# Chunked attention and a bilinear FFN on one core: x's sums ahead of ab's sums on GpSimd, one earlier transposition, one later output part

## The chip, the cores and the metric

The kernel runs on one core of a Trainium2 chip. The metric is the device time of one execution in microseconds. Before the change its median is 300.36 us over 5 runs (299.89 to 300.96).

Five engines work side by side, each through its own instructions in the order written: TensorE (PE for matmuls, PEld for the loads of the operand that stays in the array), VectorE (DVE), ScalarE (ACT), GpSimd (POOL) and SyncE (SP), which issues the DMAs. They meet through semaphores.

## The reference

Attention inside chunks of 64 tokens, then a feed-forward layer without an activation: two projections, multiplied with each other, and an output projection.

```python
q_c = q.reshape(B, H, nc, 64, D)            # B 8, H 8, S 576, D 64; k_c, v_c alike
scores = np.matmul(q_c, k_c.transpose(0, 1, 2, 4, 3)) / np.sqrt(D)
attn = np.exp(scores - scores.max(-1, keepdims=True))
attn = attn / (attn.sum(-1, keepdims=True) + 1e-09)
attn_out = np.matmul(attn, v_c).reshape(B, H, S, D)
x = attn_out.transpose(0, 2, 1, 3).reshape(B * S, H * D)   # 4608 x 512
out = ((x @ w_a) * (x @ w_b)) @ w_out       # d_ff 1536, out 4608 x 512
```

## The kernel before

The 4608 tokens are 9 blocks (`K`, 0 to 8) of 512, and 18 units (`U`) of 256; block K holds units 2K and 2K+1. The order of each engine's work is written out by hand: what is emitted first for an engine is in front in its queue.

**A unit's attention.** `load` brings q, k and v (SP), `cast` (line 211) makes them bf16, nearly always on GpSimd, and q and k are transposed: on TensorE in `transpose_pe` (line 224) for the first units, by DMA in `transpose_dma` afterwards. `bring` (line 383) is casts of q and k, loads of the next unit, DMA transpositions. Then follow `scores` (matmuls, exponentials on ACT), `sums` (matmuls with ones, logarithms on ACT), `inverse` (ACT) and `values` (line 335), whose matmuls leave attention's values in PSUM; DVE multiplies them with the inverse sums into the block's transposed `xT` (line 356, two instructions for a unit).

**The projections from block 2 on** use a seven-product scheme (Strassen and Winograd) in place of eight, for each of six groups `Group(K, i)` (line 493) of 256 columns of w_a and w_b. It needs four sums of parts of x, `s1` to `s4`: `combine_x` (line 477), on GpSimd from block 3 on, emitted in the preceding block at `i == 5`. They need both units' `xT`. A group's products `p1, p6, p2, p5, p7` run in its own iteration, `p3` and `p4` in the next one. `p6` is the first that reads a sum (`s2`). `p1`'s result is copied by ACT from PSUM bank pa to pb (line 529), and `p6` adds onto the copy. `p3` and `p4` end with DVE multiplications (line 561) that write `ab`, the product of the two projections.

**The output projection** of block K-1 runs while block K is projected, again with seven products: `OutGroup(K-1)` (line 602) has parts `(n, th)`, n from 0 to 6 and th 0 or 1, six matmuls each, in this order. It needs sums of parts of ab: `combine_ab` (line 573), on GpSimd, whose parts 0, 1 and 2 are emitted for one third `j` of the columns at a time, and part 3 for all thirds together in the next block. The part with `n == 2` has s2 of ab as the operand that is loaded into the array; its six loads take two for each third. The parts with `n` 0 and 1 add into one bank, po; between them ACT copies po to pq (line 675, after part (0, 1)), and n = 2 and 3 add onto that copy.

**The main loop** (from line 984) goes over K from 2 to 8 and over the six groups i. In one iteration, in this order: casts and `bring`s, `p1`, the preceding group's `add7` on DVE, `chunk(c0)`, the preceding group's `p3`, attention of place (K, i, 0) with `combine_x` at i = 5, `p6`, the preceding group's `p4`, `finish(last)`, `p2`, `chunk(c1)`, attention of place (K, i, 1), `p5`, `exps`, `chunk(c2)`, `p7`. `chunk(n)` emits the next n output parts; the counts stand in the table `chunks` (line 969), two entries for an iteration, c0 and then c1, or a pair (c1, c2). `finish(g)` (line 977) emits the three `combine_ab` instructions of third i - 3 when the group that it is handed has i of 3, 4 or 5. So a block's thirds of ab's sums are emitted at i = 4, at i = 5 and at i = 0 of the next block.

**Block 0** (line 814) is projected directly, in pairs of 128-column tiles: `b_of(0)`, `b_of(1)`, `a_of(0)`, `a_of(1)`; pair 4 also holds the transposition and the scores of unit 2.

Of the kernel before, what the change touches and what calls it, by code (L numbers as in the profile page):

```python
# [16 lines left out]
def kernel(  # L17
# [28 lines left out]
    NBLK = NTOK // BLK  # L46
# [41 lines left out]
    def bank(pool=None):  # L88
        if pool is None:
            pool = spread[0]  # L90
            spread.append(spread.pop(0))
        if pool is psum_b:
            pool = psum_b[0]
            psum_b.append(psum_b.pop(0))
        return pool.tile([128, 512], FP32, name=bank_names[id(pool)])
# [59 lines left out]
    def combine_wo(part, j):  # L155
        k = slice(2 * j, 2 * j + 2)
        k2 = slice(HFT + 2 * j, HFT + 2 * j + 2)
        b11, b12 = wo_sb[:, k, 0:256], wo_sb[:, k, 256:512]
        b21, b22 = wo_sb[:, k2, 0:256], wo_sb[:, k2, 256:512]
        t1, t2, t3, t4 = [t[:, k] for t in wo_t]  # L160
        o, x0, x1, op = (
            (t3, b22, b12, SUB), (t2, t3, b11, ADD), (t4, b21, t2, SUB), (t1, b12, b11, SUB)
        )[part]
        nc.gpsimd.tensor_tensor(out=o, in0=x0, in1=x1, op=op)
# [46 lines left out]
    def cast(U, names="qkv"):  # L211
        for n in names if U < NU else "":
            if U >= 4 and wo_sums:
                combine_wo(*wo_sums.pop(0))
            raw[n, U] = raw_pool.tile(
                [128, 2, H, D], BF16, name=f"{n}_raw"
            )
            eng = nc.vector if U == 0 and n != "v" else nc.gpsimd
            eng.tensor_copy(out=raw[n, U], in_=staged.pop((n, U)))
# [4 lines left out]
    def transpose_pe(U, names="qk"):  # L224
        if U not in qkt:
            qkt[U] = qkt_pool.tile([128, 2, 2, NKT, 128], BF16, name="qkt")
        for n in names:
            w = "qk".index(n)
            src = raw.pop((n, U))
            t = [bank() for _ in range(2 if U < 3 else 1)]  # L230
            tp = [
                t[i % len(t)].bitcast(BF16).rearrange("c (i m p) -> c i m p", i=2, m=NKT)[:, i]
                for i in range(2)
            ]
            for i in range(2):
                for m in range(NKT):
                    nc.tensor.transpose(
                        tp[i][:, m, :],
                        src[:, i, 2 * m:2 * m + 2, :].rearrange("p j d -> p (j d)"),
                        identity,  # L240
                    )
            dst = qkt[U][:, w].rearrange("c g m (p i) -> c i m g p", i=2)
            for i in range(2):
                on_dve = i == 0 if U in (0, 2) else w == 0 or U == 1
                cp = nc.vector.tensor_copy if on_dve else nc.scalar.copy
                cp(out=dst[:, i], in_=tp[i].rearrange("c m (g p) -> c m g p", g=2))
# [51 lines left out]
    def sums(U, halves=None, pools=(None, None)):  # L298
        E = E_of[U]
        sm = [bank(p) for p in pools]  # L300
        for cl in range(2):
            for j in range(2):
                nc.tensor.matmul(
                    sm[cl][j * 64:j * 64 + 64, :],
                    ones[cl * 64:cl * 64 + 64, :],
                    E[cl * 64:cl * 64 + 64, j].rearrange("p m g s -> p (m g s)"),
                    start=True,
                    stop=True,
                )
        ln_of[U] = sm_pool.tile([128, 2, NKT, 128], FP32, name="ln")  # L310
        rs_of[U] = ln_of[U]
        ln = ln_of[U]
        for cl in range(2):
            late_ln.append(
                lambda cl=cl: nc.scalar.activation(
                    out=ln[:, cl].rearrange("p m n -> p (m n)"), in_=sm[cl], func=AF.Ln
                )
            )
        for cl in range(1 if pools[0] else 2):
            late_ln.pop(0)()  # L320
            if halves:
                inverse(U, cl)

    def inverse(U, cl=None):

        if (U, cl) == (1, 1):
            for m in (slice(0, 2), slice(2, 4)):
                nc.scalar.activation(
                    out=rs_of[U][:, 1, m], in_=ln_of[U][:, 1, m], func=AF.Exp, scale=-1.0
                )  # L330
            return
        c = slice(0, 2) if cl is None else cl
        nc.scalar.activation(out=rs_of[U][:, c], in_=ln_of[U][:, c], func=AF.Exp, scale=-1.0)
# [49 lines left out]
    def bring(U, names="qkv"):  # L383

        if U >= NU:
            return
        cast(U, "qk")
        load(U + 1, "q" if U < 9 else "qkv")
        transpose_dma(U)
        if "v" in names:  # L390
            bring_v(U)
# [345 lines left out]
    with tc.manual_schedule(  # L737
# [72 lines left out]
        def combo():  # L810
            if combos:
                combine_w(*combos.pop(0))

        for i in range(NWP):
            pair = Pair(i) if i else first
            pair.b_of(0, (None,) if i else (1,), i == 5)
            if i == 5:
                sums(2, halves=True)
            pair.b_of(1, (None,) if i else (1,), i >= 4)
            if i == 4:  # L820
                transpose_pe(2)
                pair.copy(1)
            if i == 5:
                values(2)
                pair.copy(0)
                pair.copy(1)
            pair.a_of(0)
            if i == 4:
                scores(2)
            if 1 <= i < 5:  # L830
                combo()
            pair.a_of(1)
            if 0 <= i < 5:
                combo()
# [129 lines left out]
        def attend(K, i, n):  # L964
# [3 lines left out]
        last = None  # L968
        chunks = {
            2: (1, 1, 1, 1, 1, 2, 1, 2, 3, 0, 1, 1),  # L970
            3: (1, 1, 1, 1, 2, 1, 1, 2, 2, 0, 1, 1),
            4: (1, 0, 1, 2, 1, (1, 1), 1, 2, 2, 0, 1, 1),
            5: (1, 1, 1, 1, 1, (1, 1), 1, 2, 2, 0, 1, 1),
            NBLK - 1: (1,) * 12,
        }
# [1 line left out]
        def finish(g):  # L977

            K, i = g.K, g.i
            if K >= 2 and i >= 3:  # L980
                for part in (0, 1, 2):
                    combine_ab(K, part, i - 3, nc.vector if (K, i) == (NBLK - 1, 5) else None)

        for K in range(2, NBLK):
            for i in range(NWP):
                if i == (2 if K == 2 else 1):
                    for j in range(3):
                        combine_ab(K - 1, 3, j)
                if K == 2 and i in (1, 3):
                    bring((8, 9)[i // 2], ("qkv", "qk")[i // 2])  # L990
                elif K == 3 and i in (1, 3, 5):
                    bring(10 + i // 2, ("qkv", "qkv", "qk")[i // 2])
                elif K > 3 and i == 1:
                    bring(2 * K + 5, "qk")
                elif K > 3 and i == 2:
                    cast(2 * K + 4, "v")
                elif K > 3 and i == 3:
                    cast(2 * K + 5, "v")
                    bring(2 * K + 6, "qk")
                if i == 0:  # L1000
                    g = OutGroup(K - 1)
                    outs += [
                        lambda g=g, n=n, th=th: g.part(n, th) for n in range(7) for th in range(2)
                    ]
                now = Group(K, i)
                steps = chunks.get(K, chunks[5])[2 * i:2 * i + 2]
                c0, c1, c2 = steps[0], *(steps[1] if type(steps[1]) is tuple else (steps[1], 0))
                now.p1()
                while late_ln:
                    late_ln.pop(0)()  # L1010
                if last:
                    last.add7()
                chunk(c0)
                if K == 2 and i == 0:
                    for j in range(3):
                        combine_wo(3, j)
                if last:
                    last.p3()
                attend(K, i, 0)
                now.p6()  # L1020
                if last:
                    last.p4()
                    finish(last)
                if K == 2 and 0 < i < 4:
                    combine_w(i + 2, 3)
                if K == 2 and i == 4:
                    cast(9, "v")
                now.p2()
                chunk(c1)
                attend(K, i, 1)  # L1030
                now.p5()
                exps()
                chunk(c2)
                now.p7()
                last = now
        ends = [
            OutGroup(NBLK - 1, 0, (psum_t, psum_q, psum_c)),
            OutGroup(NBLK - 1, 1, (psum_t, psum_b, psum_a)),
# [44 lines left out]
```

## Time and profile before

| What | Value |
|---|---|
| Median of 5 runs (lowest, highest) | 300.36 us (299.89, 300.96) |
| The profiled execution's own time | 300.82 us |
| Its span, first to last instruction | 299.0 us |
| PE busy | 289.8 us, 97% |
| PEld busy | 232.6 us, 78% |
| POOL busy | 217.5 us, 73% |
| DVE busy | 197.9 us, 66% |
| ACT busy | 196.7 us, 66% |
| Granted TensorE clock | 1.00 |

The span is what the engines' instructions cover; the execution's own time is 1.8 us longer. An engine's share is an average over all stages. A row of the timeline has the start in us, the time in us, engine, line, operation, what is written and read, the shape, how many like it follow one another (their time is that of all together), and in brackets how long the engine sat idle before it and what ended that.

### The profile page before, as it was taken

How to read it: one execution, taken by the hardware profiler on the slowest of the kernel's cores; microseconds unless marked ns; L12 is line 12 of the kernel's file. 1: busy time of each engine (PE TensorE's matmuls, PEld its weight loads, DVE VectorE, ACT ScalarE, POOL GpSimd, SP SyncE). 2: the span in 40 equal slices, each digit the busy share in tenths (PEclk: the TensorE clock that was granted, in tenths of full speed). 3: DMA queues.
4: the chain of work that ended last, by engine and by line, in shares of the span. 5: the costliest groups of instructions: out<-in, count | busy, mean ns of one | idle time of the engine just before them, and what ended most of it. 6: DMA issues, size and time to landing. Idle time of an engine off the chain costs nothing.

```text
span 299.0 us, 8610 instructions
## 1 busy us (share of the span) xinstructions
PE 289.8 (97%) x3531; PEld 232.6 (78%) x3531; DVE 197.9 (66%) x312; ACT 196.7 (66%) x357; POOL 217.5 (73%) x203
## 2 busy tenths in 40 slices
PE   7799999999999999999999999999999999999995
PEld 3354478766688888887888888888888888888884
DVE  3656777867787765676466756675667576765672
ACT  2743477268587767874977687768776876566622
POOL 0557669999899499939993999299819922992660
PEclk9999999999999999999999999999999999999999
DMA  7999999999999979999999983980313001100025
GB/s 228 312 366 366 309 354 352 248 203 199 275 244 163 240 168 263 179 238 235 217 263 226 267 198 68 233 198 2 72 45 89 12 2 70 73 2 0 2 99 183
DMA packets 141159, 54.29 MB, mean 182 GB/s; under 512 B 117184, under 2 KB 135232, under 8 KB 141120
## 3 DMA queue, kind: packets, MB, share of 16 engines
q1 hardware_dynamic: 140976, 53.69, 72.9%
q8 instruction: 27, 0.44, 0.6%
q14 instruction: 12, 0.10, 0.1%
q10 hardware_dynamic: 144, 0.07, 0.1%
HBM read 37.75 MB, written 9.44 MB: 158 GB/s over the span
## 4 chain that ended last, share of the span: by engine, by line
PE 87%; SPq 3%; POOL 3%; ACT 3%; DMA 2%; issue 1%; DVE 1%; DVEq 0%; POOLq 0%
PE pb L511 18%; PE pc L511 11%; PE pa L511 11%; PE po L654 11%; PE pq L654 10%; PE pb L435 4%; PE pb L727 3%; PE pq L417 2%; PE pa L417 2%; DMA st<-in_moe_w_b_dram 2%; PE po L435 2%; PE po L417 2%; PE pt L345 2%; PE pc L417 2%; SPq L188 2%; PE pc L435 1%
## 5 line engine op out<-in xcount | busy, mean ns | idle before, releaser
L591 POOL TENSOR_TENSOR so<-ab_sb 128x512 f16<-128x512 f16 x23 | 26.6, 1156 | 42.9 <-DVE ab_sb L561 42.9
L511 PEld LDWEIGHTS <-t 128*128 128x128 f16 x504 | 48.7, 98 | 8.4 <-issue 2.8
L549 DVE TENSOR_TENSOR c_sb<-pc,v_sb 128x512 f32<-128x512 f32 x42 | 29.0, 691 | 35.6 <-ACT v_sb L522 35.6
L511 PE MATMUL pb<-s,wa 128*128 128x256 f16 x336 | 50.6, 273 | 0.1
L511 PE MATMUL pa<-xT,wb 128*128 128x256 f16 x336 | 50.4, 273 | 0.0
L654 PEld LDWEIGHTS <-ab_sb 128*128 128x128 f16 x390 | 37.8, 98 | 4.3
L522 ACT COPY u_sb<-pb 128x512 f32<-128x512 f32 x42 | 24.7, 587 | 19.4 <-PE pb L511 19.2
L561 DVE SCALAR_TENSOR_TENSOR ab_sb<-pc,c_sb 128x512 f16<-128x512 f32 x42 | 29.0, 691 | 10.8 <-PE pc L511 10.2
L511 PEld LDWEIGHTS <-wa 128*128 128x128 f16 x336 | 31.7, 98 | 5.4 <-issue 1.6
L511 PEld LDWEIGHTS <-wb 128*128 128x128 f16 x336 | 32.9, 98 | 3.9
L561 DVE SCALAR_TENSOR_TENSOR ab_sb<-pb,b_sb 128x512 f16<-128x512 f32 x42 | 29.0, 691 | 6.7 <-PE pb L511 5.7
L529 ACT COPY pb<-pa 128x512 f32<-128x512 f32 x42 | 23.9, 570 | 11.7 <-PE pa L511 11.5
L654 PEld LDWEIGHTS <-so 128*128 128x128 f16 x288 | 28.2, 98 | 3.3
L522 ACT COPY b_sb<-pa 128x512 f32<-128x512 f32 x42 | 24.9, 592 | 8.0 <-PE pa L511 8.0
L550 DVE TENSOR_TENSOR pc<-pc,u_sb 128x512 f32<-128x512 f32 x42 | 29.0, 689 | 0.0
L522 ACT COPY v_sb<-pb 128x512 f32<-128x512 f32 x42 | 24.6, 586 | 5.0 <-PE pb L511 4.9
L591 POOL TENSOR_TENSOR so<-so,ab_sb 128x512 f16<-128x512 f16 x23 | 26.6, 1155 | 1.7
L591 POOL TENSOR_TENSOR ab_sb<-ab_sb 128x512 f16<-128x512 f16 x23 | 26.9, 1171 | 0.0
L356 DVE TENSOR_TENSOR xT<-pt,ln 128x512 f16<-128x512 f32 x31 | 20.2, 686 | 9.3 <-PE pt L345 7.2
L591 POOL TENSOR_TENSOR so<-ab_sb,so 128x512 f16<-128x512 f16 x23 | 26.1, 1161 | 0.0
L511 PE MATMUL pb<-s,t 128*128 128x256 f16 x168 | 25.3, 273 | 0.8 <-POOL s L491 0.7
L511 PE MATMUL pc<-xT,t 128*128 128x256 f16 x168 | 25.2, 273 | 0.1
(148 smaller groups left out, 585.0 us busy)
## 6 DMA issues: line engine op xcount, KB each, us to landing
st<-in_v_dram SPq DMA_DIRECT2D x32, 256.0 KB, 4.5
out_dram<-o_sb SPq DMA_DIRECT2D x30, 256.0 KB, 2.5
st<-in_k_dram SPq DMA_DIRECT2D x22, 256.0 KB, 4.1
st<-in_q_dram SPq DMA_DIRECT2D x20, 256.0 KB, 3.9
st<-in_q_dram SPq DMA_DIRECT2D x6, 512.0 KB, 5.9
st<-in_moe_w_b_dram SPq DMA_DIRECT2D x6, 512.0 KB, 7.5
st<-in_moe_w_a_dram SPq DMA_DIRECT2D x6, 512.0 KB, 7.1
st<-in_moe_w_out_dram SPq DMA_DIRECT2D x6, 512.0 KB, 6.4
```

The lines of the kernel that those rows point to most:

```text
L356: nc.vector.tensor_tensor(out=x.rearrange("p m (g c s) -> p m g c s", g=2, c=2)[:, m, :, cl, :], in0=av[cl][:, m], in1=rs[:, cl, m].rearra ...
L417: nc.tensor.matmul(ps[n], w_ab[n, i][:, kt, o:o + 128], xT[:, kt, c0:c1], start=(kt == 0), stop=(kt == NKT - 1),)
L435: nc.tensor.matmul(t[:, c], w_ab[n, i][:, kt, o:o + 128], x_tiles[0][:, kt, c], start=(kt == 0), stop=(kt == NKT - 1),)
L511: nc.tensor.matmul(t[:, h * 256:h * 256 + 256], w[:, kt, h * 128:h * 128 + 128], x[:, kt], start=start and h == 0 and kt == 0, stop=h == 1 ...
L522: nc.scalar.copy(out=t, in_=src)
L529: nc.scalar.copy(out=self.B, in_=self.A)
L549: nc.vector.tensor_tensor(out=self.c, in0=self.C, in1=self.v, op=ADD)
L550: nc.vector.tensor_tensor(out=self.C, in0=self.C, in1=self.u, op=ADD)
L561: nc.vector.scalar_tensor_tensor(out=self.dst[:, :, c0:c0 + 256], in0=t.rearrange("p (h n) -> p h n", h=2), scalar=AB_SCALE, in1=o.rearran ...
L591: (eng or nc.gpsimd).tensor_tensor(out=o, in0=x0, in1=x1, op=op)
L654: nc.tensor.matmul(t[:, c0:c0 + 256][:, cols], a[:, kt, th * 128:th * 128 + 128], w[:, kt, cols], start=n in (0, 4) and first and kt == 0, ...
L727: nc.tensor.matmul(out_ps[K, tg], ab_tiles[K][:, ft, tg * 128:tg * 128 + 128], wo_sb[:, ft], start=(ft == 0), stop=(ft == NFT - 1),)
```

## The change

Three edits. First, in blocks 2 to 7 the first third of ab's sums is no longer emitted at i = 4 but at i = 5, together with the second third and after `combine_x` of the next block; and the cast of v of unit 9, which stood at i = 4 of block 2, follows `combine_x` too. The last block keeps its order. Second, in block 0's pair 4 the q of unit 2 is transposed on TensorE between the two b products, and its k where both were. Third, in block 4 the second output part goes from i = 1 to i = 0, behind `p5`, and iteration 1 has one part before and one after the attention in place of one and two.

```diff
@@ -816,9 +816,11 @@
             pair.b_of(0, (None,) if i else (1,), i == 5)
             if i == 5:
                 sums(2, halves=True)
+            if i == 4:
+                transpose_pe(2, "q")
             pair.b_of(1, (None,) if i else (1,), i >= 4)
             if i == 4:
-                transpose_pe(2)
+                transpose_pe(2, "k")
                 pair.copy(1)
             if i == 5:
                 values(2)
@@ -969,7 +971,7 @@
         chunks = {
             2: (1, 1, 1, 1, 1, 2, 1, 2, 3, 0, 1, 1),
             3: (1, 1, 1, 1, 2, 1, 1, 2, 2, 0, 1, 1),
-            4: (1, 0, 1, 2, 1, (1, 1), 1, 2, 2, 0, 1, 1),
+            4: (1, (0, 1), 1, 1, 1, (1, 1), 1, 2, 2, 0, 1, 1),
             5: (1, 1, 1, 1, 1, (1, 1), 1, 2, 2, 0, 1, 1),
             NBLK - 1: (1,) * 12,
         }
@@ -1020,11 +1022,14 @@
                 now.p6()
                 if last:
                     last.p4()
-                    finish(last)
+                    if K == 2 and i == 5:
+                        cast(9, "v")
+                    if i == 5 and K < NBLK - 1:
+                        finish(before)
+                    if i != 4 or K == NBLK - 1:
+                        finish(last)
                 if K == 2 and 0 < i < 4:
                     combine_w(i + 2, 3)
-                if K == 2 and i == 4:
-                    cast(9, "v")
                 now.p2()
                 chunk(c1)
                 attend(K, i, 1)
@@ -1032,7 +1037,7 @@
                 exps()
                 chunk(c2)
                 now.p7()
-                last = now
+                before, last = last, now
```

## The prediction

> **What bounds the kernel now.** I read the page, the chain of waits, PE's own waits, and then timelines around each edit. The chain says 87% PE, and busy PE is 97%.
>
> ```profile
> PE 87%; SPq 3%; POOL 3%; ACT 3%; DMA 2%; issue 1%; DVE 1%; DVEq 0%; POOLq 0%
> ...
> PE pb L511 <- POOL s L491: 0.7, 1, 0.7
> ...
> 138.88 1.15 POOL L491 TENSOR_TENSOR s<-s,xT 128x512 f16<-128x512 f16 x1
> ...
> 140.08 0.60 PE L511 MATMUL pb<-s,t 128*128 128x256 f16 x4 [0.70 <-POOL s L491]
> ```
>
> After the start-up, PE's matmuls follow one another at their own pace (0.109 us from one 256-column matmul to the next), so what a matmul waits is lost for good, and what no matmul waits for costs nothing. From start to start I find three places after 17 us that this change touches. **C**, at 139.1: p6 of block 4's first group waits for s2 of x; the group before it starts at 138.78 and needs 0.44, so p6 could start at 139.22; it starts at 140.08, 0.86 late. **A**, at 34.5: unit 2's scores wait for ACT's copy of the transposed k. **D**, at 144.8: p6 of block 4's second group waits for ACT's copy pb<-pa; p3 before it starts at 144.05, so 144.49 would do: 0.31 late.
>
> Ahead of each block, POOL's row tells what sets C:
>
> ```profile
> 132.22 1.16 POOL L591 TENSOR_TENSOR so<-ab_sb 128x512 f16<-128x512 f16 x1 [4.78 <-DVE ab_sb L561]
> ...
> 135.66 1.05 POOL L219 CAST q_raw<-st 128x1024 bf16<-128x1024 f32 x1
> 136.63 1.05 POOL L219 CAST k_raw<-st 128x1024 bf16<-128x1024 f32 x1
> 137.64 1.16 POOL L491 TENSOR_TENSOR s<-xT 128x512 f16<-128x512 f16 x1
> ```
>
> POOL sits idle for 4.78 us with the casts of unit 12 queued behind ab's first third, which waits for DVE; then come two casts, then x's sums.
>
> **What the Trainium skill says.** "PSUM — Partial Sum Buffer", section "Engine vs sequencer instructions": the queues of ScalarE, VectorE and GpSimd are strict FIFO. The trace agrees: the 4.78 us idle above, with k of unit 12 landed at 132.9. The same page, section "PSUM bank collisions raise a hardware error", has PSUM guarded by bank: so a matmul that adds into po must let ACT's copy of po end first; in the trace part (1, 0) of block 4 starts at 146.1, after the copy of 145.15 to 145.76. "Perfetto Trace Analysis", section "Identifying the Most-Contended Engine", warns that matmul busy time isn't distance from the limit; hence start to start above (weight loads are busy 78% here).
>
> **Part 1, x's sums first (POOL).** Nothing is added; 3 instructions of 1.16 (ab's first third) go behind 4 of 1.16 (x's sums).
>
> *Block 3 to 4.* The casts of unit 12 no longer stand behind the third. Its q landed at 131.0 and k at 132.9: casts end at about 134.0, x's sums need xT (DVE done at 133.55), so they start near 134.1 and s2 is done 2.4 later, at 136.5, against the need at 139.22. C goes: **-0.86**. All nine ab instructions end no later than before, since the casts use the idle time. DMA: the transpositions of unit 12 stand behind loads on SP that end at 143.1, so an earlier cast doesn't move them.
>
> *The other blocks.* No casts stand there, and here the edit has a price: x's sums wait for the second unit's xT, later than the DVE multiplication that ab's third waited for.
>
> ```profile
> 102.22 1.16 POOL L591 TENSOR_TENSOR so<-ab_sb 128x512 f16<-128x512 f16 x1 [0.48 <-DVE ab_sb L561]
> ...
> 115.93 1.15 POOL L591 TENSOR_TENSOR so<-so,ab_sb 128x512 f16<-128x512 f16 x1
> ...
> 102.27 1.29 DVE L356 TENSOR_TENSOR xT<-pt,ln 128x512 f16<-128x512 f32 x2
> ...
> 117.25 0.75 PEld L654 LDWEIGHTS <-so 128*128 128x128 f16 x7
> ```
>
> Rows 1 and 2: POOL at the end of block 2 starts at 102.22 and ends s2 of ab's last third at 115.93 + 1.15 = 117.08, without a pause. Row 3: xT is done at 103.56, so x's sums can start at 103.65 (0.09 from DVE's end to POOL's start, as at 132.13 to 132.22). The same set of instructions, v9's cast included, starts 1.43 later with no slack behind, so that s2 ends at 118.51. Row 4: output part (2, 0) of the next block loads it. The loads' records carry POOL waits on the first, third and fifth of six; the fifth, the last third, is at 117.25 + 4 x 0.11 = 117.69. After C's example (POOL's end 140.03, matmul 140.08) 0.05 is to be added: 118.56. Margin before 0.61, delay 1.43 + 0.05: **+0.87** lost in block 3.
>
> The same sum elsewhere:
>
> ```profile
> 178.37 0.64 PEld L654 LDWEIGHTS <-so 128*128 128x128 f16 x6
> ...
> 208.11 0.64 PEld L654 LDWEIGHTS <-so 128*128 128x128 f16 x6
> ...
> 237.87 0.64 PEld L654 LDWEIGHTS <-so 128*128 128x128 f16 x6
> ...
> 266.56 0.64 PEld L654 LDWEIGHTS <-so 128*128 128x128 f16 x6
> ```
>
> Fifth loads at 178.80, 208.55, 238.31, 267.00. s2 ended at 177.27, 207.02, 236.75, 266.19; POOL's start moves from 163.38, 193.13, 222.88, 252.32 to xT's end + 0.09 (164.81, 194.56, 224.30, 253.75), by 1.42 or 1.43 each time. New ends + 0.05: 178.75, 208.50, 238.22, 267.67. Blocks 5 to 7 just make it, by 0.05 to 0.09 (I take 0; up to 0.15 each if a row is longer). Block 8 has no attention, so PE comes sooner: 0.67 late, **+0.67**. What else is 1.43 later on POOL: part 3 of ab's sums (block 5: ends 181.7, read from 189.4), the casts and, behind them on SP, transpositions (unit 15 from 182.7, read by scores at 193.0), the next unit's loads, and stores (issued from 195.2, their buffer wanted near 207). All have over 1.4 of cover; without it a late transposition would stop PE directly.
>
> v9's cast moves with the rest; v9 is first read by block 3's values at 131.8, over 20 us later.
>
> **Part 2, q of unit 2 earlier.** Same 16 transposing matmuls and 4 copies. ACT now copies k's half at 33.69, right behind q's copy (33.09, 0.75). With q done one product earlier (ready near 32.2) k's copy starts when its matmuls end, 33.34 + 0.20 (as q's: 32.89 to 33.09) = 33.54, and ends at 34.30, scores 34.35 against 34.50: **-0.15**; from 0 to -0.21, where only the step into 64x64 matmuls is left (0.09 elsewhere). The b product behind q is covered: its ACT copy is emitted after k's, and a_of(1) needs it at 36.0.
>
> **Part 3, part (0, 1) of block 4 behind p5.**
>
> ```profile
> 143.04 0.60 ACT L522 COPY v_sb<-pb 128x512 f32<-128x512 f32 x1
> 143.50 0.64 ACT L285 ACTIVATE E<-pb 128x512 bf16<-128x512 f32 x1
> 144.18 0.57 ACT L529 COPY pb<-pa 128x512 f32<-128x512 f32 x1
> 144.66 0.60 ACT L315 ACTIVATE ln<-pt 128x512 f32<-128x512 f32 x1
> 145.15 0.61 ACT L675 COPY pq<-po 128x512 f32<-128x512 f32 x1
> ...
> 142.53 0.60 PE L511 MATMUL pc<-s,t 128*128 128x256 f16 x4
> ```
>
> ACT works without pause here, 0.48 from start to start. In this trace's clock: p5 ends its issue at 142.53, part (0, 1) takes to 143.18, p7 to 143.62, p1 to 144.05, and part (1, 0), now first, wants po. But the copy pq<-po stands on ACT behind the exponential: starts 143.98, ends 144.59, so (1, 0) starts at 144.64, 0.58 late. Then p3 145.30 to 145.73, and p6 finds pb<-pa done (144.46 to 145.03). Before, p6 started at 144.80 with one part of 0.65 fewer in front, that is 145.45: **+0.28**. If the copy waits for the exponential's end, as pb<-pa does (144.18), +0.48; if ACT were done in time, -0.31.
>
> **Sum.** -0.86 + 0.87 + 0.67 - 0.15 + 0.28 = +0.81, with 0.04 for blocks 5 to 7: +0.85. Span 299.02 + 0.85 = 299.87; with the 1.80 around it 301.67 for a profiled execution like this one, which lay 0.46 above the median: about 301.2.
>
> **Rivals.**
> 1. *ACT is in time for po*: the copy goes ahead of the exponential or is hidden by p7 and p1; D is removed instead of traded. Sum +0.26: 300.6. Against it: ACT's rows without pause.
> 2. *Ab's last third isn't late* (the other side): s2's third is ready when part (2, 0) loads it in blocks 3 and 8. It decides on POOL's delay: under 0.56 in block 3 and 0.76 in block 8 nothing is lost, -1.54 on the sum, -0.69: 299.7. For it: POOL's spans are rough, and waits may be placed otherwise. Against: the FIFO and no slack between 102.22 and 117.08.
> 3. *Blocks 5 to 7 slip as well*, by 0.15 each, and the copy of po drains: +0.45 + 0.2: 301.9.
> 4. *Part 1 leaves C*: k of unit 12 lands over 2 us later than now, so the casts block x's sums: +0.86 more, 302.1. Landing at 132.9 speaks against it.
>
> **Chances.** Forecast 0.58, rival 1 0.17, rival 2 0.10, rival 3 0.11, rival 4 0.04. 0.2% (0.6 us) is about what a measurement tells from no change: rival 2 is faster, 0.10; rival 1 and a fifth of the forecast's spread are within, 0.28; the rest slower, 0.62. Range 299.9 to 302.0: it leaves out rival 2 and the far end of 4.
>
> **What would show it.** Right: no wait of PE for `s` near 139; waits of PEld for POOL `so` of 0.8 in block 3 and 0.6 in block 8, near 118 and 268; a wait for ACT `pq` of 0.5 near 144; scores of unit 2 at 34.35. Wrong: part (2, 0) in blocks 3 and 8 without a wait (rival 2), no ACT wait before (1, 0) (rival 1), or waits of PE for transposed q and k, which I count at nothing.

## The result, and the profile after

The changed kernel takes 301.37 us in the median of 43 runs, the kernel before 300.71 in 80 runs beside it. The ratio is 1.0028, 95% interval 1.0021 to 1.0034: +0.84 us (0.63 to 1.02), against a forecast of +0.85. The ratio is not the quotient of the two medians, which lie 0.66 us apart; where a change in us stands beside a ratio below, it is worked out from the ratio.

The profiled execution after has a span of 298.9 us, no longer than before (299.0), and that needs a word: it is the shortest of the 43 (300.73 us), and its first weights landed sooner (14.63 and not 15.51), so that block 0's first product into bank po starts at 18.74 and not at 19.50. From that product on, the changed kernel is 0.66 us longer in its records. Below, "from the mark" means: from this product on, against the kernel before.

The chain of waits by engine, on the page of the changed kernel:

```profile
PE 81%; POOL 9%; SPq 3%; ACT 2%; DMA 2%; issue 1%; DVE 1%; DVEq 0%; POOLq 0%
```

POOL held 3% of the chain and now holds 9%: GpSimd decides in more places. PE's own waits say which (total us, times, longest; the start-up's are left out):

```profile
PE pq L654 <- POOL so L591: 1.0, 2, 0.6
...
PE po L654 <- ACT pq L675: 0.5, 1, 0.5
```

The wait for `s` of x (0.7, near 139) is not there any more. Two waits for ab's sums and one for ACT's copy are new. The loads for output part (2, 0) on TensorE's load side (PEld's timeline), in block 3 and in block 8:

```profile
116.28 0.42 PEld L654 LDWEIGHTS <-so 128*128 128x128 f16 x4
117.63 0.77 PEld L654 LDWEIGHTS <-so 128*128 128x128 f16 x8 [0.92 <-POOL so L591]
...
265.91 0.43 PEld L654 LDWEIGHTS <-so 128*128 128x128 f16 x4
267.00 0.11 PEld L654 LDWEIGHTS <-so 128*128 128x128 f16 x2 [0.66 <-POOL so L591]
```

Four loads go, the fifth waits for ab's last third. GpSimd's timeline of the changed kernel has the reason, at the end of block 2, of block 3 and of block 7:

```profile
102.72 1.16 POOL L491 TENSOR_TENSOR s<-xT 128x512 f16<-128x512 f16 x1 [3.28 <-DVE xT L356]
...
116.42 1.15 POOL L591 TENSOR_TENSOR so<-so,ab_sb 128x512 f16<-128x512 f16 x1
...
131.35 1.04 POOL L219 CAST q_raw<-st 128x1024 bf16<-128x1024 f32 x1 [3.42 <-DMA st<-in_q_dram]
133.31 1.04 POOL L219 CAST k_raw<-st 128x1024 bf16<-128x1024 f32 x1 [0.91 <-DMA st<-in_k_dram]
134.31 1.15 POOL L491 TENSOR_TENSOR s<-xT 128x512 f16<-128x512 f16 x1
...
253.08 1.15 POOL L491 TENSOR_TENSOR s<-xT 128x512 f16<-128x512 f16 x1 [11.15 <-DVE xT L356]
...
265.79 1.15 POOL L591 TENSOR_TENSOR so<-so,ab_sb 128x512 f16<-128x512 f16 x1
```

In block 2 POOL is idle until xT is there and then works without a pause until ab's last third is done at 117.57; the load comes 0.06 later. Block 7 has the same picture: the third is done at 266.94, the load for block 8's part comes at 267.00. In block 3 the casts use what was idle time, and x's sums start 3.3 us sooner than the 137.64 of before.

Block 4's second group, where part (1, 0) now comes right behind `p1`, on ACT and then on PE:

```profile
142.49 0.64 ACT L285 ACTIVATE E<-pb 128x512 bf16<-128x512 f32 x1
142.98 0.64 ACT L675 COPY pq<-po 128x512 f32<-128x512 f32 x1
143.50 0.61 ACT L529 COPY pb<-pa 128x512 f32<-128x512 f32 x1
```

```profile
142.60 0.60 PE L511 MATMUL pa<-xT,wb 128*128 128x256 f16 x4
143.68 0.81 PE L654 MATMUL po<-wo,ab_sb 128*128 128x256 f16 x6 [0.47 <-ACT pq L675]
```

Four matmuls take 0.44 to issue, so part (1, 0) could start at 143.04; it starts at 143.68, after the copy ends at 143.62.

The waits of TensorE from the mark on at which the two kernels differ, by the starts of its matmuls, in us lost ("by the starts" below means this way of counting; of A, 0.09 is the step from wide to 64x64 matmuls, which such places lose elsewhere too):

| Place | Before | After |
|---|---|---|
| A: scores of unit 2 | 0.30 | 0.12 |
| C: p6 of block 4's first group, s2 of x | 0.86 | none |
| D: p6 of block 4's second group, pb<-pa | 0.31 | none |
| Block 4, part (1, 0), po | none | 0.63 |
| Block 3, part (2, 0), ab's last third | none | 0.80 |
| Block 8, part (2, 0), ab's last third | none | 0.55 |
| Sum | 1.47 | 2.10 |

The difference, 0.63, is the 0.66 of the records from the mark but for 0.03.

### The profile page after: what moved, and what is told of

It is laid out like the page before. It is cut to its first block, busy times and chain, and to the rows that moved or that the text cites. A ratio compares the mean times of both kernels' runs of the same rounds, so it can differ in the third digit from the quotient of the medians.

```text
span 298.9 us, 8612 instructions
## 1 busy us (share of the span) xinstructions
PE 290.0 (97%) x3531; PEld 232.6 (78%) x3531; DVE 200.1 (67%) x312; ACT 196.9 (66%) x357; POOL 217.1 (73%) x203
## 4 chain that ended last, share of the span: by engine, by line
PE 81%; POOL 9%; SPq 3%; ACT 2%; DMA 2%; issue 1%; DVE 1%; DVEq 0%; POOLq 0%
PE pb L511 16%; PE pc L511 10%; PE pa L511 10%; PE pq L654 10%; PE po L654 9%; POOL so L591 5%; PE pb L435 4%; POOL s L491 3%; PE pb L727 3%; PE pq L417 2%; PE pt L345 2%; PE pa L417 2%; PE po L435 2%; PE pc L435 2%; PE po L417 2%; PE pc L417 2%
## 5 line engine op out<-in xcount | busy, mean ns | idle before, releaser
L491 POOL TENSOR_TENSOR s<-xT 128x512 f16<-128x512 f16 x12 | 13.8, 1154 | 33.0 <-DVE xT L356 33.0
L219 POOL CAST q_raw<-st 128x1024 bf16<-128x1024 f32 x17 | 17.9, 1053 | 10.7 <-DMA st<-in_q_dram 10.7
```

The lines of the kernel that those rows point to most:

```text
L491: (eng or nc.vector).tensor_tensor(out=o, in0=x0, in1=x1, op=op)
```

## The experiments

The theory is the prediction's: TensorE sets the pace, each wait at a named place is lost in full, GpSimd's wait for xT makes ab's last third late, and ACT's queue makes part (1, 0) of block 4 late. Rivals stand with each run. Ratios are to the kernel before on the same chip.

### Part 1 alone

The changed kernel without its second and third edit:

```diff
-            if i == 4:
-                transpose_pe(2, "q")
...
-                transpose_pe(2, "k")
+                transpose_pe(2)
...
-            4: (1, (0, 1), 1, 1, 1, (1, 1), 1, 2, 2, 0, 1, 1),
+            4: (1, 0, 1, 2, 1, (1, 1), 1, 2, 2, 0, 1, 1),
```

> Part 1 alone (GpSimd's new order in blocks 2 to 7); the transposition and the output part stay as in the kernel before. My theory: the wait for s2 of x near 139 is gone (-0.86), output part (2, 0) waits for ab's last third in block 3 (0.80 in the matmuls' starts) and block 8 (0.55), the copy pb<-pa still holds up the second group of block 4 (0.31), and no wait for po. Sum +0.49 us against the kernel before. Rival, that the moved output part alone makes the loss: no waits for so, 0.9 us faster than before.

Measured: ratio 1.0010 (0.9994 to 1.0025), +0.30 us, not to be told from no change by its times, nor from the +0.49 expected; the rival's 0.9 us faster lies outside. PE's waits for ab's sums:

```profile
PE pq L654 <- POOL so L591: 2.1, 3, 1.1
```

Three waits, not two, so the rival falls by the records too. Block 8 has its 0.55 as expected, and C is gone. But block 3 waits 1.31 and block 4, for which I had counted nothing, 0.76. GpSimd's timeline of this kernel, end of block 2 and of block 3:

```profile
103.74 1.04 POOL L219 CAST k_raw<-st 128x1024 bf16<-128x1024 f32 x1 [3.67 <-DMA st<-in_k_dram]
104.74 1.15 POOL L491 TENSOR_TENSOR s<-xT 128x512 f16<-128x512 f16 x1
...
136.00 1.04 POOL L219 CAST k_raw<-st 128x1024 bf16<-128x1024 f32 x1 [0.89 <-DMA st<-in_k_dram]
137.00 1.16 POOL L491 TENSOR_TENSOR s<-xT 128x512 f16<-128x512 f16 x1
```

The profiled execution took 303.19 us, the longest of the 22, and lies 3.07 above the kernel before from the mark. In it k of unit 9 landed at 103.62 (100.58 in the profile of before, 98.28 in that of the change), and k of unit 12 was late too. Unit 9's cast stands ahead of everything in both orders, so of block 3's 1.31 the half-microsecond over 0.80 is the load's and not part 1's (nor is a wait of 0.94 at 77.9 for a transposed k, ahead of the edit's first place). Block 4's 0.76 I put down to part 1: in the old order ab's first third went ahead of unit 12's casts, in the new one all nine ab instructions stand behind them. That is read from the queue; no run has the old order with such a late load. If it is right, part 1's price depends on when a load lands, and my sum had it from one execution.

### Part 3 alone

```diff
-            4: (1, 0, 1, 2, 1, (1, 1), 1, 2, 2, 0, 1, 1),
+            4: (1, (0, 1), 1, 1, 1, (1, 1), 1, 2, 2, 0, 1, 1),
```

> Part 3 alone (output part (0, 1) of block 4 behind p5). My theory: the wait of 0.31 for pb<-pa is traded for one of 0.63 for po behind ACT's copy, +0.33 us, and the 0.86 for s2 of x stays. Rival, that the copy would be in time if part 1 didn't crowd the place: the 0.31 goes and nothing comes, -0.31 us.

Measured: 1.0013 (0.9995 to 1.0031), +0.39 us, by its times not to be told from no change; from the mark +0.33, the number expected. PE's waits:

```profile
PE pb L511 <- POOL s L491: 0.7, 1, 0.7
...
PE po L654 <- ACT pq L675: 0.5, 1, 0.5
```

The wait for s2 stays (0.86 by the starts), the one for pb<-pa is gone, and 0.63 for po has come. The rival predicted no wait for po and 0.31 less; the records refuse it.

### Part (1, 0) of block 4 later

On the changed kernel:

```diff
-            4: (1, (0, 1), 1, 1, 1, (1, 1), 1, 2, 2, 0, 1, 1),
+            4: (1, (0, 1), 0, 2, 1, (1, 1), 1, 2, 2, 0, 1, 1),
```

> The changed kernel with part (1, 0) of block 4 moved behind p2 of the second group, together with (1, 1), so that nothing asks for po early. My theory: ACT's queue is the cause, so the wait moves to p6, which finds pb<-pa 0.6 to 0.7 late; the time is that of the changed kernel within 0.1 us. Rival, that only the place of the part that needs po is bad: the 0.63 goes and nothing comes in its place.

Measured: 1.0045 (1.0031 to 1.0059), some 0.5 us above the changed kernel's 1.0028, with intervals that just touch; what would make that difference isn't in the profile, which has +0.73 from the mark where the changed kernel has +0.66. PE's waits:

```profile
PE pb L511 <- ACT pb L529: 0.5, 1, 0.5
```

The wait for po became one of 0.68 (by the starts) for pb<-pa. So the place of part (1, 0) alone isn't to blame, and the rival falls. But not all of the 0.68 is ACT's queue: a group that has no part between p1 and p6 loses 0.37 there even where ACT is idle before the copy (the first of the two runs below that move part (2, 0) later). For part (1, 0) itself the queue is shown by the rows above, where the copy of po follows ACT's other work without a pause.

### One ACT instruction fewer ahead of pb<-pa

On the kernel before: in block 4 the logarithm of the first sums goes behind the copy, and the inverse one group later.

```diff
...
-                at(K, 0, 1, sums_beside(psum_t, psum_t), U)
+                at(K, 0, 1, sums_beside(psum_t, psum_t, now=0), U)
...
-            at(K, 1, 0, inverse, U)
+            at(K, 2 if K == 4 else 1, 0, inverse, U)
```

> The kernel before with one ACT instruction fewer ahead of the copy pb<-pa in block 4: the logarithm of unit 10's first sums goes behind that copy, and the inverse of these sums from the second to the third group. My theory: ACT's queue is what makes the second group wait, the copy starts 0.48 sooner and the 0.31 goes: -0.31 us, with up to 0.15 given back at p5. Rival: the copy waits for the exponential that reads the same bank, whatever stands ahead, and at least 0.2 of the wait stays.

Measured: 0.9989 (0.9975 to 1.0004). By the starts, the 0.31 at p6 is gone and 0.16 has come at part (1, 0), which waits for the copy of po, one place further back in ACT's queue: net 0.15, the half that the expectation allowed for, at another place than it named. The times don't tell it from no change, and from the mark the profile has 0.09 less up to TensorE's last matmul and 0.11 more up to the end. ACT's timeline:

```profile
143.33 0.60 ACT L285 ACTIVATE E<-pb 128x512 bf16<-128x512 f32 x1
143.97 0.57 ACT L529 COPY pb<-pa 128x512 f32<-128x512 f32 x1
```

The rival (the exponential in the same bank keeps at least 0.2 at p6) falls. What it names is there, though: the copy starts as the exponential ends (143.93), as in the kernel before (144.14 and 144.18). It costs p6 nothing once both come earlier.

### Part 1 only where it pays, with part 2

On the kernel before:

```diff
-                    finish(last)
+                    if i == 5 and K == 3:
+                        finish(before)
+                    if i != 4 or K != 3:
+                        finish(last)
```

and `before, last = last, now` at the loop's end, and the second edit of the change.

> The kernel before with part 1 in block 3 only, and part 2. My theory: the only gains of the change without its prices, -0.86 for s2 of x and -0.17 for the scores of unit 2, -1.03 us, ratio 0.9966; part (2, 0) of blocks 3 and 8 without a wait, the 0.31 at block 4's second group stays. Rival, that what part 1 saves at s2 of x comes back as another wait in block 4: no faster than -0.2 us.

Measured: 0.9964 (0.9949 to 0.9979), -1.08 us, and from the mark -0.89, where -1.03 was expected. All that the view of PE's waits lists for this kernel:

```profile
PE pc L101 <- DVE warm_in L80: 1.3, 1, 1.3
PE po L274 <- DVE qkt L246: 0.8, 1, 0.8
PE pt L237 <- DVE q_raw L219: 0.6, 1, 0.6
PE po L345 <- POOL v_raw L219: 0.2, 1, 0.2
```

These four are of the start-up. No wait for `s`, none for `so`; by the starts, which also show waits that the view leaves out, the 0.31 at block 4's second group is there. What part 1 saves at s2 of x doesn't come back. This version beats both kernels: 299.86 us in the median of 16 runs, against 300.69 beside it.

### The output parts moved in place of GpSimd's order, twice

The changed kernel, with the part that reads ab's last third later on TensorE. First try:

```diff
-            3: (1, 1, 1, 1, 2, 1, 1, 2, 2, 0, 1, 1),
+            3: (1, 1, 1, 1, 0, 3, 1, 2, 2, 0, 1, 1),
...
-            NBLK - 1: (1,) * 12,
+            NBLK - 1: (1, 1, 1, 1, 0, 2, 1, 1, 1, 1, 1, 1),
```

> The changed kernel with output part (2, 0) later in block 3 and block 8: in the third group of both, the parts that stood at the first place stand at the second one, some 1.7 us later on TensorE; GpSimd's order is that of the change. My theory: ab's last third is there in time, both waits go, 1.35 us less than the changed kernel, 0.7 us faster than the kernel before. Rival, that TensorE loses this time to something else in these blocks (a copy, a buffer): the time stays as that of the changed kernel.

Measured: 1.0044 (1.0026 to 1.0062), where 1.35 us less than the change was expected. If anything it is slower than the change: the intervals overlap, and from the mark it is +1.41. PE's waits:

```profile
PE pq L654 <- ACT uo_sb L683: 0.7, 1, 0.7
...
PE pb L511 <- ACT pb L529: 0.4, 2, 0.2
```

Both waits for `so` are gone, as the theory has it, but my edit brought its own: (2, 0), (2, 1), (3, 0) in a row in block 3 leave ACT no time to copy pq between n = 2 and n = 3 (0.85 by the starts), and a group without a part between p1 and p6 waits 0.37 for the copy pb<-pa, in both blocks, though ACT is idle for 0.24 before that copy. As a test it decides nothing; the second try avoids both:

```diff
-            3: (1, 1, 1, 1, 2, 1, 1, 2, 2, 0, 1, 1),
+            3: (1, 1, 1, 0, 1, 2, 2, 2, 2, 0, 1, 1),
...
-            NBLK - 1: (1,) * 12,
+            NBLK - 1: (1, 1, 1, 0, 1, 2, 1, 1, 1, 1, 1, 1),
```

> The changed kernel with output part (2, 0) again later in blocks 3 and 8, now by moving part (1, 1) one place back in their second group, (2, 0) and (2, 1) to the second place of their third group; no group loses the part that stands between p1 and p6, and no part follows (2, 1) at once. GpSimd's order is that of the change. My theory: the loads of ab's last third come some 1.7 us later, both waits go (0.80 and 0.55) and at most 0.1 each comes at p5; about 1.2 us less than the changed kernel. Rival, that any place costs TensorE the same here: the time of the changed kernel.

Measured: 1.0000 (0.9984 to 1.0016), so 0.84 us less than the change; from the mark -0.30 against +0.66, that is 0.96 less. Expected was 1.2. No wait for `so` is left; by the starts a new one of 0.22 stands at p7 of block 3's second group, where the part that used to separate p2 from p5 is missing: p7 starts at 115.41, after DVE's multiplication out of the same bank has ended at 115.35. GpSimd's order is that of the change here: with the reader later, its two waits, 0.80 and 0.55, are gone. The rest of the difference between 1.35 and 0.96, some 0.17, I have not placed.

### Part (2, 0) of block 8 earlier

```diff
-            NBLK - 1: (1,) * 12,
+            NBLK - 1: (1, 1, 1, 2, 0, 1, 1, 1, 1, 1, 1, 1),
```

> The changed kernel with part (2, 0) of block 8 one place earlier, three products (1.31 us) sooner on TensorE. My theory: the wait for ab's last third grows by what the load comes sooner, from 0.55 to 1.86, +1.3 us on the changed kernel. Rival, that the wait there is a fixed price of that place or of the order on GpSimd: it stays at 0.55.

Measured: 1.0087 (1.0058 to 1.0116), 1.8 us more than the change. PEld's waits:

```profile
PEld L654 <- POOL so L591: 2.9, 2, 2.0
```

The wait in block 8 is 1.87 by the starts, 1.32 more than in the change, for a reader that comes three products, 1.31, earlier in TensorE's order. Another 0.38 comes at a group that now has no part between p1 and p6, as in the first try above. So the wait in block 8 is a deadline missed, not a fixed price.

### The cast of v9, ahead of x's sums and behind everything

First ahead, where it stood before the change:

```diff
-                    if K == 2 and i == 5:
-                        cast(9, "v")
...
+                if K == 2 and i == 4:
+                    cast(9, "v")
```

> The changed kernel with the cast of v9 back at the fifth group of block 2, ahead of x's sums, in the 3.3 us in which GpSimd is idle there. My theory: the 14.85 us from x's first sum to ab's last third shrink by one cast, 0.99, more than the load is late (0.91), so block 3's wait is gone or under 0.1, block 8's stays at 0.55: 0.75 us less than the changed kernel. Rival, that GpSimd was never the cause in block 3: the wait stays at 0.80.

Measured: 1.0008 (0.9993 to 1.0023), 0.6 us below the change where 0.75 was expected, with intervals that just overlap. In the profiled execution, which took 302.48 us where the median of the 20 is 300.63, the wait in block 3 stayed, 0.79, against the expectation. GpSimd's timeline:

```profile
101.47 1.04 POOL L219 CAST k_raw<-st 128x1024 bf16<-128x1024 f32 x1 [2.34 <-DMA st<-in_k_dram]
104.20 1.04 POOL L219 CAST v_raw<-st 128x1024 bf16<-128x1024 f32 x1 [1.69 <-PE pc L511]
105.20 1.15 POOL L491 TENSOR_TENSOR s<-xT 128x512 f16<-128x512 f16 x1
```

The row names PE, which was done; by the DMA's records v9 landed at 104.05 in this execution, as late as xT (104.15), so that its cast filled no idle time. In the change's own profile v9 landed at 100.22, 2.4 ahead of xT, so that there the cast would have fitted; how often that is so isn't known. The other way doesn't depend on the landing:

```diff
-                    if K == 2 and i == 5:
+                    if K == 3 and i == 1:
                         cast(9, "v")
```

> The changed kernel with the cast of v9 after ab's last third (second group of block 3) in place of before its first. My theory: the work between xT and ab's last third is shorter by that cast, 0.99, whenever v9 lands; the wait of block 3 (0.80 in the matmuls' starts, 0.91 in the load) goes, 0.8 us less than the changed kernel, unless k of unit 9 lands after xT. Rival, that block 3's wait isn't set by how much stands on GpSimd ahead of that third: it stays.

Measured: 1.0001 (0.9978 to 1.0024), 0.8 us below the change, with intervals that just overlap; from the mark +0.02, 0.64 less than the change. In GpSimd's timeline the last third's s2 now ends 13.88 us after x's first sum starts, and not 14.85:

```profile
102.90 1.16 POOL L491 TENSOR_TENSOR s<-xT 128x512 f16<-128x512 f16 x1 [1.18 <-DVE xT L356]
...
115.63 1.15 POOL L591 TENSOR_TENSOR so<-so,ab_sb 128x512 f16<-128x512 f16 x1
```

Block 3's wait is gone, block 8's is there (0.59). That the wait is set by how much stands on GpSimd between xT and the last third is shown by this run; the one before it only agrees with it once v9's landing is known.

### Part 2 alone

The second edit of the change on the kernel before.

> Part 2 alone (q of unit 2 transposed between the two b products). My theory: the scores of unit 2 start 0.17 sooner and all after them, -0.17 us, hardly to be told from no change in the times, but to be seen in the trace. Rival, that the earlier q only moves the wait to the b product's copy or to the values of unit 2: 0.

Measured: 0.9998 (0.9985 to 1.0011). In the profiled execution, the longest of the 14 (302.00 us; the median is 300.55), the scores of unit 2 did not come sooner: they lose 0.37 by the starts, where the kernel before loses 0.30. The timelines of GpSimd and DVE, then PE's:

```profile
31.69 1.04 POOL L120 CAST wa<-st 128x1024 f16<-128x1024 f32 x1 [0.31 <-DMA st<-in_moe_w_a_dram]
...
31.90 1.11 DVE L135 TENSOR_TENSOR t<-wb,t 128x512 f16<-128x512 f16 x1
...
34.25 0.73 DVE L246 COPY qkt<-pt 128x512 bf16<-128x512 bf16 x1
34.87 0.71 DVE L246 COPY qkt<-pa 128x512 bf16<-128x512 bf16 x1
```

```profile
35.73 0.45 PE L274 MATMUL pt<-qkt 64*64 64x64 bf16 x32 [0.20 <-DVE qkt L246]
```

I had followed ACT's half of the copies only. DVE makes the other half, and here it comes to them late, behind sums of weights. One of these takes 1.11 us beside a cast on GpSimd; in the profile of before, sums of this shape take 0.41 to 1.37. "SBUF — State Buffer" of the Trainium skill, section "SBUF: two separate sides", says that a DVE instruction with two SBUF inputs and a GpSimd instruction that reads SBUF share a port pair, which one of them holds for its whole length. The durations agree with that: in the fourteen profiles together, the 40 such sums with no GpSimd instruction beside them took 0.41 to 0.43, the 408 others 0.40 to 1.42. But no run took the overlap away. Of the ten profiled kernels with this edit, the scores lose 0.12 to 0.15 in six and 0.22 to 0.37 in four; the four kernels profiled without it lose 0.28 to 0.30. So the edit gains its 0.15 where DVE is in time, and little or nothing where it isn't. Each of those four profiles is of an execution longer than its kernel's median, and only one of the six is, so that four in ten need not be the usual share.

### What paid, together

Part 1 in block 3 alone, part 2, and the ACT edit of block 4.

> What paid, together: the kernel before with part 1 in block 3 only, part 2, and the logarithm and inverse of unit 10 later on ACT in block 4; no moved output part. My theory: -0.89 (both measured in one kernel) and -0.15 for the ACT edit, -1.04 us, ratio 0.9965. Rival, that the ACT edit is worth nothing beside part 1: as the kernel with part 1 in block 3 and part 2 alone, -0.9.

Measured: 0.9976 (0.9962 to 0.9990), -0.72 us, faster than before, but not faster than the same without the ACT edit (0.9964, 0.9949 to 0.9979); the intervals overlap. From the mark it is -0.83. By the starts it has the 0.16 at part (1, 0) as expected and 0.35 at the values of unit 2, which stand at 37.4, far ahead of the edit, and which b3_p2's profile does not show. Whether the ACT edit is worth its 0.15 stays open.

## Why the prediction was right

The forecast held in sign and in size (+0.85; +0.84 measured), and the mechanism of its four large terms was right. That the two agree to a hundredth is luck: the terms as the profile has them add up to 0.63, and of those that were off all but one were sized too high, by up to 0.12. They are:

- **C, -0.86**: measured, to the hundredth. x's sums started at 134.31 where I had 134.1, because k landed a little later.
- **Block 3, +0.87, and block 8, +0.67**: right mechanism, shown by four runs (the reader later, the reader earlier, one cast fewer in front, part 1 in block 3 alone), sized too high: 0.80 and 0.55. The loads were late by nearly what I had worked out, 0.91 and 0.65 against 0.87 and 0.67. But the matmul behind such a load loses one slot less here: in the flow a load runs 0.11 ahead of its matmul, and after a wait both start together (load and matmul at 117.63). I had charged the load's delay to the matmul.
- **Blocks 5 to 7, +0.04**: nothing; from the second group of block 4 to the end of block 7 the two kernels keep their distance from the mark to 0.03.
- **A, -0.15**: -0.18 in the profile of the change, but it fails in some executions. The step that failed is the cover: I named the ACT copies and not DVE's, which come to their half behind the sums of weights.
- **Part 3, +0.28**: +0.33; the copy of po started 0.49 behind the exponential, without draining it, as I had taken it. The copies themselves took 0.03 to 0.04 longer.
- **What I costed at nothing**: the DMA transpositions, loads and stores behind GpSimd's casts, and v9's cast. No wait for q or k transposed by DMA is in PE's waits after. The reader of v9 was in time, as I had written, but the cast stands between xT and ab's last third: with it elsewhere, block 3's wait is gone (the run that casts v9 behind everything).
- **Rival 4** (loads of unit 12 land later) got 0.04 of the chances, with the wrong victim. In the run of part 1 alone the late k stopped no p6; it came with ab's last third late for block 4 (0.76). I had written that all nine ab instructions end no later than before; that holds only while unit 12 lands in time.

The sum of the measured terms is 0.63 and the runs say 0.84, 0.63 to 1.02, with medians 0.66 apart. So there may be no gap between the two. If there is one, late landings like that one could fill it, but how often they come isn't known from one profile for each kernel; this part stays open. The three parts measured alone (+0.30, +0.39 and, for part 2, -0.06) add up to 0.63 as well, each of them within its noise.

## What to carry to other kernels

In an in-order queue, moving work that waits for A ahead of work that waits for B pays only if A comes first or the idle time is used by something else; compare the two releases block by block, and carry the delay to every reader behind, with its margin. Here the same edit gained 0.86 us where casts could fill the gap and lost 1.35 where they couldn't. With the edit in that one block only, part 2 and no part 3, the kernel is 0.36% faster than before, where the whole change made it 0.28% slower. Before a piece of TensorE's work is moved, ask which copy on another engine it was hiding: taking the part from between p1 and p6 cost 0.37 or 0.38 at three places, and 0.68 at a fourth, where ACT was behind as well.

## What the runs showed that I had not expected

- At both waits for ab's sums, the matmul behind the load lost about one slot (0.11 us) less than the load was late: 0.80 for 0.91, 0.55 for 0.65.
- Between executions of nearly the same program, the same load landed at 98.28, 100.58 and 103.62 (k of unit 9). GpSimd's order decides how much stands behind such a load. Each profile is one execution: five of the fourteen are the longest of their kernel's runs or the next to longest, and that of the change is the shortest.
- Sums of two fp16 tiles on DVE, 128x512, took up to 1.42 us beside GpSimd instructions, over three times the 0.41 to 0.43 with none beside them.
